# Forming w_out·phi with phi as the stationary operand in four column groups, and one more product that adds and transposes

## The chip, the cores and the metric

The kernel runs on one core of one Trainium2 chip. The metric is the device time of one execution in microseconds (us), lower is better. The matmul engine is called PE in the rows (PEld is its weight load), the vector engine DVE, the scalar engine ACT, GpSimd POOL, and the queue that issues DMAs SP.

## The reference

Three layers follow each other on 2304 tokens (4 sequences of 576) of 512 features. First comes an attention with 8 heads of 64, of which four see a local window of 32 positions and four every 32nd position; its output is `x`. Then a feed-forward layer and a soft mixture of experts:

```python
h = x @ w_in                                  # 2304x512 @ 512x2048
g = h * (1.0 / (1.0 + np.exp(-1.702 * h)))
x = g @ w_out                                 # 2048x512
logits = x @ phi                              # 512x32
d = softmax(logits, axis=0)                   # over the tokens
slot_input = d.T @ x                          # 32x512
# each of 8 experts: two products on its 4 rows of slot_input -> slot_out
c = softmax(logits, axis=1)                   # over the 32 slots
return c @ slot_out
```

The layer's output `x` (2304x512) is never needed by itself: `logits = g @ (w_out @ phi)`, and `slot_input = (d.T @ g) @ w_out`. The kernel therefore forms the small product `wp = w_out @ phi` (2048x32) once, and uses it as the weights of the logits.

## The kernel before, in words

The five chunks of tokens (`CHUNKS`, four of 512 and one of 256) go through a loop of 80 steps, `steps`, each step one chunk `c` and one of 16 slices `f` of 128 of the 2048 hidden features (`moe_step`, line 344). A step runs `gemm1` (line 304): twelve matmuls of 512 columns into `h` (line 311), then a tanh on ACT (line 314) and a product on DVE (line 315) that give `g`, kept in the slots of `gT`. Every fourth step `logits` (line 325) multiplies four slices of `g` by `wp` (line 330, four column groups of 32 side by side). `g_transpose` (line 333) turns `g` in DVE for the later product with the softmax weights.

While chunk 0 runs (steps 0 to 15), the weights are also prepared. `load_w(i + 2)` (line 251) reads the raw weights of a slice, which come as 64-bit numbers, and makes float32 of them: an ACT pass (line 259), a POOL pass (line 260) and three DVE passes (lines 261 to 263), for `w_in` (k = 0) and `w_out` (k = 1) each. `split(i + 1)` (line 266) cuts `w_in` into two parts, by an ACT cast (line 270) and a POOL subtraction (line 271), whose result `wi` the twelve matmuls of the step use. `wo_transpose(i + 1)` (line 273) transposes the slice of `w_out`, by four matmuls with the identity (line 278, the tile `wot`) and an ACT copy (line 280) to `woT`, four blocks of 128x128 with the 512 features on the partitions. `wo_phi(i)` (line 282) is what changes: it multiplies these four blocks, as the stationary operand, by `phs`, the four blocks of 128x32 of phi, as the moving one, and adds the four products in PSUM (line 286). An ACT instruction halves the 128x32 result into `wp[:, f]` (line 287).

The attention of the next sequence runs among these steps as well (`attention_steps`, resumed once a step through `side`): scores `s` (line 161, 64x64 operands), mask, maximum and exponential on DVE and ACT (lines 164 to 179), a POOL multiplication (line 182), transposes `ptp` (line 197) and products with the values `av` (line 216), whose results ACT and DVE move to `x` (lines 241 and 242).

The order of the work on each engine is not the order of the code: a scheduler lists the instructions by priority and readiness when the program is built. Each engine works through its list strictly in that order. The PSUM tiles `wp`, `wot`, `s`, `ptp` and `av` share one pool of five (`mtile`, line 65); `h` has two tiles of its own, and `lg` one. `sel` (line 85) is a constant 128x32 matrix whose row r has a one in column r mod 32.

Of the kernel before, what the change touches and what calls it, by code (L numbers as in the profile page):

```python
# [9 lines left out]
F32 = mybir.dt.float32  # L10
# [11 lines left out]
NS = NE * SPE  # L22
# [8 lines left out]
NF = FF // 128  # L31
# [10 lines left out]
def tile_kernel(ctx: ExitStack, tc: tile.TileContext, lqk, lv, sqk, sv, wraw, phi, wexp, cst, out):  # L42
    nc = tc.nc
    P = 128
# [16 lines left out]
    rawp = raw_es.enter_context(tc.tile_pool(name="rawp", bufs=3, side="right"))  # L61
# [3 lines left out]
    def mtile(name):  # L65
        return ps_m.tile([P, 512], F32, tag="m", name=name)
# [18 lines left out]
    sel = rep[:, :NS]  # L85
# [4 lines left out]
    phs = keep.tile([P, 4, NS], F32, name="phs")  # L90
    ca = keep.tile([P, NT // 128, NS], F32, name="ca")
    wp = keep.tile([P, NF, NS], F32, name="wp")
# [158 lines left out]
    def load_w(f):  # L251
        for k in range(2):
            if (f, k) not in raws:
                load_raw(f, k)
        for k in range(2):
            raw = raws.pop((f, k))
            t = rawp.tile([P, 512], F32, tag="wc", name=f"wc_{f}_{k}", bufs=4)
            u = t.bitcast(U32)
            nc.scalar.activation(t, raw[:, :, 1].bitcast(F32), AF.Abs)  # L259
            nc.gpsimd.tensor_scalar(t, t, F64_LARGE, F64_SMALL, op0=ALU.min, op1=ALU.max)  # L260
            nc.vector.tensor_scalar(u, u, 3, 0x3FFFFFF8, op0=ALU.logical_shift_left, op1=ALU.bitwise_and)  # L261
            nc.vector.scalar_tensor_tensor(u, raw[:, :, 1], 0xC0000000, u, op0=ALU.bitwise_and, op1=ALU.bitwise_or)  # L262
            nc.vector.scalar_tensor_tensor(u, raw[:, :, 0], 29, u, op0=ALU.logical_shift_right, op1=ALU.bitwise_or)  # L263
            conv[f, k] = t

    def split(f):
        if f % 2 == 0:
            wis[f // 2] = wip.tile([P, 2, 2, 512], F32R, tag="wi", name=f"wi_{f // 2}")
        w, t = wis[f // 2][:, f % 2], conv.pop((f, 0))
        nc.scalar.copy(w[:, 0], t)  # L270
        nc.gpsimd.tensor_tensor(w[:, 1], t, w[:, 0].bitcast(F32), op=ALU.subtract)  # L271

    def wo_transpose(f):
        t = conv.pop((f, 1))
        nc.sync.dma_start(wo_scr[f], t)
        tp = mtile(f"wot_{f}")
        for kt in range(4):
            nc.tensor.transpose(tp[:, 128 * kt:128 * kt + 128], t[:, 128 * kt:128 * kt + 128], ident)
        woT[f] = rawp.tile([P, 4, 128], F32, tag="woT", name=f"woT_{f}", bufs=1)
        nc.scalar.copy(woT[f].rearrange("p k f -> p (k f)"), tp)  # L280

    def wo_phi(f):
        t = woT.pop(f)
        pw = mtile(f"wp_{f}")[:, :NS]
        for kt in range(4):
            nc.tensor.matmul(pw, t[:, kt, :], phs[:, kt, :], start=kt == 0, stop=kt == 3)  # L286
        nc.scalar.mul(wp[:, f, :], pw, 0.5)

    steps = [(c, f) for c in range(len(CHUNKS)) for f in range(NF)]
    lgs, gs = {}, {}  # L290
# [13 lines left out]
    def gemm1(c, f):  # L304
        N = CHUNKS[c][1]
        x, w = xt[c], wis[f // 2][:, f % 2]
        h = ps_h.tile([P, 512], F32, tag="h", name=f"h_{c}_{f}")
        n = 0
        for kt in range(4):
            for we, xe in ((0, 0), (0, 1), (1, 0)):  # L310
                nc.tensor.matmul(h[:, :N], w[:, we, 128 * kt:128 * kt + 128], x[xe][:, kt, :N], start=n == 0, stop=n == 11)  # L311
                n += 1
        g = g_slot(c, f)
        nc.scalar.activation(g[:, :N], h[:, :N], AF.Tanh, scale=0.851)  # L314
        nc.vector.scalar_tensor_tensor(g[:, :N], g[:, :N], 1.0, h[:, :N], op0=ALU.add, op1=ALU.mult)  # L315
        gs[c, f] = g
# [8 lines left out]
    def logits(c, f0):  # L325
        N = CHUNKS[c][1]
        if f0 == 0:
            lgs[c] = ps_lg.tile([P, 512], F32, tag="lg", name=f"lg_{c}")
        for j in range(4):
            nc.tensor.matmul(lgs[c][32 * j:32 * j + 32, :N], wp[:, f0 + j, :], gs[c, f0 + j][:, :N], start=f0 == 0, stop=f0 == NF - 4)  # L330
            g_used(c, f0 + j)

    def g_transpose(c, f):
        N = CHUNKS[c][1]
        if c < 4:
            assert f not in taken
            taken.add(f)
        nc.vector.transpose(t_slots(c)[:, f, :N], gs[c, f][:, :N])  # L338
        g_used(c, f)
# [4 lines left out]
    def moe_step(i):  # L344
        c, f = steps[i]
        if i + 2 < NF:
            load_w(i + 2)
        if 0 < i < NF:
            wo_phi(i)
        for s in list(side):  # L350
            if next(s, True):
                side.remove(s)
        if i + 1 < NF:
            split(i + 1)
        if c == 0 or f >= TFROM:
            for _ in range(1 if c == 0 else 2):
                if todo and (c or todo[0][1] not in taken):
                    g_transpose(*todo.pop(0))
        while todo and todo[0][0] < c and todo[0][1] not in taken:
            g_transpose(*todo.pop(0))  # L360
        gemm1(c, f)
        if i + 1 < NF:
            wo_transpose(i + 1)
        if i and f % 4 == 0:
            pc, pf = steps[i - 4]
            logits(pc, pf)
            if f == 0:
                side.append(post(pc))
        todo.append((c, f))
# [147 lines left out]
    for n, _ in enumerate(attention_steps(0)):  # L517
        if n in (8, 12):
            load_w(n // 4 - 2)
        if n == 10:  # L520
            split(0)
    wo_transpose(0)
    wo_phi(0)
    busy_t[0] = cs.bitcast(BF16)[:, :512]
    early_es.close()
# [6 lines left out]
    for i, (c, f) in enumerate(steps):  # L532
        if f == 0 and c < 3:
            side.append(attention_steps(c + 1))
            next(side[-1])
        if (c, f) == (1, 0):
            raw_es.close()
            accp = acc_es.enter_context(tc.tile_pool(name="accp", bufs=1))
            sp_["p"] = accp
            acc = accp.tile([P, 4, 512], F32, name="acc")  # L540
            more = accp.tile([P, 3, 512], F32, name="more")
            slots.update({NF + 3 + k: more[:, k] for k in range(3)})
        if (c, f) == (3, 2):
            att_es.close()
            e1p = ctx.enter_context(tc.tile_pool(name="e1p", bufs=4, side="right"))
            for _ in range(4):
                load_ex(e1p, "e")
            for e in (1, 0, 1):
                load_ex(xp, f"x{e}")
        if (c, f) == (4, 1):  # L550
            for e in range(2):
                load_ex(xp, f"x{e}")
        moe_step(i)
        if (c, f) == (4, 4):
            for k in range(2):
                load_ex(None, gx_tile())
        if c == 4 and f % 2:
            load_ex(wip, "wi")
# [236 lines left out]
```

## Time and profile before

| | |
|---|---|
| median of 3 runs | 445.32 us (443.66 to 446.91) |
| the profiled execution, own time | 447.54 us |
| its span, first to last instruction | 445.7 us |
| mean granted TensorE clock in it | 0.973 |
| PE, DVE, ACT, POOL busy | 419.5, 263.4, 191.3, 77.4 us |

The rows further down are of that one execution; times in them are us from the start of its span, unless they are means of one instruction, which are ns. A row of PE gives records: one float32 matmul leaves two records (two passes). A record lasts from the start of an instruction to its end, and those of PE overlap, since the next one enters while the last one's results still drain.

### The profile page before, as it was taken

To read this page: it belongs to the slowest core of one execution; us is meant where nothing else is said; L and a number is where in the kernel's file an instruction comes from. 1 tells how busy PE (TensorE), PEld (TensorE's weight loads), DVE (VectorE), ACT (ScalarE), POOL (GpSimd) and SP (SyncE) were. 2 spreads that over 40 slices of the span, in tenths; PEclk is the share of its full clock that TensorE was granted. 3 is DMA by queue.
4 is the path that set the end of the run, shared out by engine and by line. 5 is a ranking of instruction groups with operands and counts; after the bars stand their busy time and mean duration, and the time that the engine had idled before them with its cause. 6 is when DMAs were issued, how large, how long until landed. Compare 5 with 4: busy or idle time off the path is not lost.

```text
span 445.7 us, 9998 instructions
## 1 busy us (share of the span) xinstructions
PE 419.5 (94%) x4056; PEld 294.1 (66%) x4056; DVE 263.4 (59%) x564; ACT 191.3 (43%) x623; POOL 77.4 (17%) x96
## 2 busy tenths in 40 slices
PE   8977999998879999999999999999999999899965
PEld 4546786766547776777775777776777796243655
DVE  2689899988975555555656556546544664431212
ACT  2785676756645553554552436331222222120312
POOL 0444445445451100010110001000000000010000
PEclk9999999999999999999999999999999999899985
DMA  8856667584762130212402101680002899879998
GB/s 244 352 162 221 217 194 275 175 287 159 248 219 65 57 95 4 92 36 79 166 25 73 37 2 37 225 341 1 1 0 89 304 368 329 338 290 427 421 351 249
DMA packets 25614, 80.90 MB, mean 181 GB/s; under 512 B 2144, under 2 KB 9440, under 8 KB 21472
## 3 DMA queue, kind: packets, MB, share of 16 engines
q1 hardware_dynamic: 25568, 80.26, 50.9%
q8 instruction: 32, 0.52, 0.5%
q14 instruction: 14, 0.11, 0.1%
HBM read 71.34 MB, written 8.91 MB: 180 GB/s over the span
## 4 chain that ended last, share of the span: by engine, by line
PE 73%; DVE 9%; DMA 6%; ACT 5%; POOL 4%; issue 2%; SPq 0%; ACTq 0%; POOLq 0%
PE h L311 41%; PE u L423 5%; PE s L161 4%; PE lg L330 4%; DMA out<-gT 4%; PE hp L627 3%; PE ptp L197 3%; DVE wc L262 3%; PE op L657 2%; PE wp L286 2%; PE av L216 2%; ACT ts L179 2%; DVE wc L263 2%; POOL wi L271 2%; DMA qk<-lqk 2%
## 5 line engine op out<-in xcount | busy, mean ns | idle before, releaser
L311 PE MATMUL h<-x,wi 128*128 128x512 f32 (+1 forms) x960 | 223.8, 380 | 5.9 <-POOL wi L271 3.5
L311 PEld LDWEIGHTS h<-x,wi 128*128 128x128 f32 x960 | 162.2, 189 | 53.4 <-issue 13.8
L315 DVE SCALAR_TENSOR_TENSOR gT<-gT,h 128x512 f32<-128x512 f32 (+1 forms) x64 | 40.5, 633 | 61.8 <-ACT gT L314 61.2
L314 ACT ACTIVATE gT<-h 128x512 f32<-128x512 f32 (+1 forms) x64 | 35.5, 555 | 69.7 <-PE h L311 69.4
L179 ACT ACTIVATE ts<-ts,nmx 128x64 f32<-128x64 f32 (+1 forms) x120 | 41.6, 349 | 29.1 <-DVE nmx L174 28.9
L182 POOL TENSOR_TENSOR ts<-ts,sm 128x384 f32<-128x384 f32 (+2 forms) x32 | 28.1, 880 | 138.7 <-DVE sm L181 63.7
L338 DVE STREAM_TRANSPOSE gT<-gT 128x512 f32<-128x512 f32 (+1 forms) x64 | 41.0, 649 | 0.8
L260 POOL TENSOR_SCALAR wc<-wc 128x512 f32<-128x512 f32 x32 | 24.1, 755 | 34.9 <-ACT wc L259 34.8
L262 DVE SCALAR_TENSOR_TENSOR wc<-raw,wc 128x512 uint32<-128x512 uint32 x32 | 28.0, 878 | 0.3
L263 DVE SCALAR_TENSOR_TENSOR wc<-raw,wc 128x512 uint32<-128x512 uint32 x32 | 26.6, 832 | 0.1
L161 PE MATMUL s<-qk 64*64 64x96 f32 (+1 forms) x552 | 26.0, 242 | 0.5 <-DMA qk<-lqk 0.5
L161 PEld LDWEIGHTS s<-qk 64*64 64x64 f32 x552 | 22.0, 138 | 6.6 <-issue 4.7
L330 PE MATMUL lg<-gT,wp 128*32 128x512 f32 (+1 forms) x128 | 26.4, 564 | 0.0
L271 POOL TENSOR_TENSOR wi<-wc,wi 128x512 fp32r<-128x512 f32 x16 | 22.5, 1407 | 14.7 <-ACT wi L270 14.3
L261 DVE TENSOR_SCALAR wc<-wc 128x512 uint32<-128x512 uint32 x32 | 17.2, 537 | 11.9 <-POOL wc L260 11.8
L201 ACT COPY pt<-ptp 96x384 f32<-96x384 f32 (+1 forms) x34 | 15.1, 483 | 20.3 <-PE ptp L197 20.1
L241 ACT CAST x<-av 128x320 fp32r<-128x320 f32 (+20 forms) x54 | 19.0, 398 | 10.5 <-DVE x L242 9.1
L180 DVE TENSOR_SCALAR sm<-sm 128x5 f32<-128x5 f32 (+2 forms) x32 | 7.1, 223 | 26.5 <-ACT ts L179 26.5
L423 PE MATMUL u<-gT,dT 32*32 32x512 f32 x576 | 21.1, 623 | 1.9 <-DVE z L398 1.9
L179 ACT ACTIVATION_READ_ACCUMULATOR ts<-ts,nmx 128x1 f32 x120 | 22.6, 188 | 0.0
L197 PE MATMUL ptp<-cs,ts 128*96 128x128 f32 (+1 forms) x120 | 18.1, 285 | 4.0 <-POOL ts L182 3.0
L259 ACT ACTIVATE wc<-raw 128x512 f32<-128x512 f32 x32 | 21.6, 678 | 0.7 <-DMA raw<-wraw 0.7
(120 smaller groups left out, 469.8 us busy)
## 6 DMA issues: line engine op xcount, KB each, us to landing
ex<-wexp SPq DMA_DIRECT2D x28, 1024.0 KB, 7.8
raw<-wraw SPq DMA_DIRECT2D x32, 512.0 KB, 3.7
qk<-lqk SPq DMA_DIRECT2D x8, 592.0 KB, 4.7
wo_scr<-wc SPq DMA_DIRECT2D x16, 256.0 KB, 2.4
ex<-wo_scr SPq DMA_DIRECT2D x4, 1024.0 KB, 9.5
gT<-wexp SPq DMA_DIRECT2D x4, 1024.0 KB, 5.9
qk<-sqk SPq DMA_DIRECT2D x6, 604.0 KB, 4.4
v<-lv SPq DMA_DIRECT2D x8, 432.0 KB, 4.4
```

Source lines behind the costliest of these rows:

```text
L161: nc.tensor.matmul(sp[hs, u], t[hs, qo:qo + 64], t[hs, ko + qo:ko + qo + nk], start=not early, stop=not early or u == nt - 1)
L179: nc.scalar.activation(ts[:, u], src[:, u], AF.Exp, scale=sc, bias=nmx[:, u:u + 1], accum_out=sm[:, u:u + 1])
L197: nc.tensor.transpose(ptp[:nk, u - a], src, ident)
L262: nc.vector.scalar_tensor_tensor(u, raw[:, :, 1], 0xC0000000, u, op0=ALU.bitwise_and, op1=ALU.bitwise_or)
L263: nc.vector.scalar_tensor_tensor(u, raw[:, :, 0], 29, u, op0=ALU.logical_shift_right, op1=ALU.bitwise_or)
L271: nc.gpsimd.tensor_tensor(w[:, 1], t, w[:, 0].bitcast(F32), op=ALU.subtract)
L311: nc.tensor.matmul(h[:, :N], w[:, we, 128 * kt:128 * kt + 128], x[xe][:, kt, :N], start=n == 0, stop=n == 11)
L314: nc.scalar.activation(g[:, :N], h[:, :N], AF.Tanh, scale=0.851)
L315: nc.vector.scalar_tensor_tensor(g[:, :N], g[:, :N], 1.0, h[:, :N], op0=ALU.add, op1=ALU.mult)
L330: nc.tensor.matmul(lgs[c][32 * j:32 * j + 32, :N], wp[:, f0 + j, :], gs[c, f0 + j][:, :N], start=f0 == 0, stop=f0 == NF - 4)
L338: nc.vector.transpose(t_slots(c)[:, f, :N], gs[c, f][:, :N])
L423: nc.tensor.matmul(us[a][32 * j:32 * j + 32, :].rearrange("p (t f) -> p t f", f=32), dT[q, 32 * b:32 * b + 32], gT[q, :, 32 * b:32 * b + 3 ...
```

## The change

`wo_phi` now loads a 128x32 block of phi as the stationary operand and streams the 128x128 block of `woT`. Each of the four blocks goes to a column group and to 32 PSUM partitions of its own, so the four products are not added: the result is 128x128, four transposed partial sums one below the other. ACT halves it into a new tile `wpT`. A new function `wo_phi_sum` then makes `wp[:, f]` by one product of `wpT` (stationary) with `sel`, which adds the four parts and transposes them, into a PSUM tile `wq` of the same pool, and by an ACT copy of 128x32. It is called one step later than the `wo_phi` of its slice, for the last slice in the first step of chunk 1.

```diff
+    wpT = {}
+
     def wo_phi(f):
         t = woT.pop(f)
-        pw = mtile(f"wp_{f}")[:, :NS]
+        pw = mtile(f"wp_{f}")[:, :P]
         for kt in range(4):
-            nc.tensor.matmul(pw, t[:, kt, :], phs[:, kt, :], start=kt == 0, stop=kt == 3)
-        nc.scalar.mul(wp[:, f, :], pw, 0.5)
+            nc.tensor.matmul(pw[32 * kt:32 * kt + 32], phs[:, kt, :], t[:, kt, :], start=True, stop=True)
+        wpT[f] = rawp.tile([P, P], F32, tag="wpT", name=f"wpT_{f}", bufs=2)
+        nc.scalar.mul(wpT[f], pw, 0.5)
+
+    def wo_phi_sum(f):
+        pw = mtile(f"wq_{f}")[:, :NS]
+        nc.tensor.matmul(pw, wpT.pop(f), sel, start=True, stop=True)
+        nc.scalar.copy(wp[:, f, :], pw)
...
         if 0 < i < NF:
             wo_phi(i)
+        if i <= NF and i:
+            wo_phi_sum(i - 1)
         for s in list(side):
```

The scheduler makes a new order from this. On PE, in the place of step 12 (`h_12`) of the kernel before, the product `wp` stands behind all of `h_12` and behind a logits matmul `lg`:

```order
L311 MATMUL h_12_1552<-x_0_302,wi_1477 128x512 x2
L278 MATMUL wot_1497<-cs,wc_1_1355 128x128 x4
L311 MATMUL h_12_1552<-x_0_303,wi_1477 128x512
L311 MATMUL h_12_1552<-x_0_302,wi_1477 128x512 x2
L311 MATMUL h_12_1552<-x_0_303,wi_1477 128x512
L311 MATMUL h_12_1552<-x_0_302,wi_1477 128x512
L330 MATMUL lg_983<-gT,wp 32x512
L286 MATMUL wp_1520<-phs,woT_1502 128x32 x4
L161 MATMUL s_3_1_1526<-qk_3_1367 64x64 x10
```

In the changed kernel the four `wp` matmuls (line 288) and the `wq` of the slice before (line 294) stand in the middle of `h_12`:

```order
L278 MATMUL wot_1542<-cs,wc_1_1392 128x128 x4
L319 MATMUL h_12_1601<-x_0_302,wi_1522 128x512 x2
L319 MATMUL h_12_1601<-x_0_303,wi_1522 128x512
L319 MATMUL h_12_1601<-x_0_302,wi_1522 128x512
L288 MATMUL wp_1565<-woT_1547,phs 32x128 x4
L294 MATMUL wq_1572<-cs,wpT_1485 128x32
L161 MATMUL s_3_1_1575<-qk_3_1408 64x64 x10
L319 MATMUL h_12_1601<-x_0_302,wi_1522 128x512
L319 MATMUL h_12_1601<-x_0_303,wi_1522 128x512
```

So `wp`, and the scores `s` behind it, have moved ahead of the rest of `h_12` and of `lg`. On ACT, in the same place, the kernel before has the tanh of `h_12` and the halving of `wp` ahead of the cast of `w_in` (line 270):

```order
L280 COPY woT_1502<-wot_1497 128x512
L314 ACTIVATE gT<-h_12_1552 128x512
L287 ACTIVATE wp<-wp_1520 128x32
L270 CAST wi_1477<-wc_0_1427 128x512
L259 ACTIVATE wc_0_1508<-raw_0_1504 128x512
```

In the changed kernel both new evictions stand ahead of that cast, and the tanh (line 322) behind it:

```order
L280 COPY woT_1547<-wot_1542 128x512
L259 ACTIVATE wc_1_1474<-raw_1_1466 128x512
L241 CAST x_2_897<-av_2_0_1490 128x18x4
L290 ACTIVATE wpT_1570<-wp_1565 128x128
L295 COPY wp<-wq_1572 128x32
L241 CAST x_2_897<-av_2_1_1491 128x14x4
L270 CAST wi_1522<-wc_0_1468 128x512
L322 ACTIVATE gT<-h_12_1601 128x512
L259 ACTIVATE wc_0_1553<-raw_0_1549 128x512
```

What ACT has to do before the cast is thus no longer the tanh of the whole step, but one eviction more.

## Rows read from the trace of the kernel before

**Rows 1.** The page: totals of engines, and busy tenths in 40 slices.

```profile
PE 419.5 (94%) x4056; PEld 294.1 (66%) x4056; DVE 263.4 (59%) x564; ACT 191.3 (43%) x623; POOL 77.4 (17%) x96
...
PE   8977999998879999999999999999999999899965
...
DVE  2689899988975555555656556546544664431212
```

**Rows 2.** Windows of 10 us, 40 to 150: busy time by engine, clock, DMA.

```profile
core 0: us, PE busy (x) PEld busy (x) DVE busy (x) ACT busy (x) POOL busy (x), PEclk, DMA share, GB/s
...
110.00:120.00 10.00, 8.82 (x84) 5.76 (x83) 10.00 (x19) 7.35 (x25) 5.94 (x6) 1.00 0.67 215
...
sum 110.00, PE 102.06 PEld 74.09 DVE 93.90 ACT 68.44 POOL 47.90; mean PE 9.28 PEld 6.74 DVE 8.54 ACT 6.22 POOL 4.35
```

**Rows 3.** The chain, pieces from 119 to 136: start, us, what.

```profile
120.92 1.02 PE wp L286 x8
...
122.75 1.29 POOL wi L271
...
128.09 1.02 PE wp L286 x8
```

**Rows 4.** The chain from 40 to 146, by line, share of it.

```profile
by line: PE h L311 22.5%; PE wp L286 9.5%; PE s L161 7.5%; POOL wi L271 7.2%; DVE wc L263 6.2%; DVE wc L262 6.1%; issue 5.2%; PE wot L278 5.1%; PE lg L330 4.6%; ACT ts L179 3.2%; PE ptp L197 3.1%; ACT wc L259 3.0%; POOL ts L182 2.4%; ACT pt
```

**Rows 5.** PE in order of time around two `wp` groups: start, us, records.

```profile
65.38 0.86 PE L311 MATMUL h<-x,wi 128*128 128x512 f32 x3
66.08 1.03 PE L286 MATMUL wp<-phs,woT 128*128 128x32 f32 x8
...
119.87 1.04 PE L330 MATMUL lg<-gT,wp 128*32 128x512 f32 x2
120.84 1.08 PE L286 MATMUL wp<-phs,woT 128*128 128x32 f32 x8
```

**Rows 6.** PE in order of time, single records at changes of tile shape.

```profile
93.73 0.39 PE L311 MATMUL h<-x,wi 128*128 128x512 f32 x1
94.05 0.62 PE L330 MATMUL lg<-gT,wp 128*32 128x512 f32 x1
...
94.50 0.59 PE L330 MATMUL lg<-gT,wp 128*32 128x512 f32 x1
95.03 0.50 PE L311 MATMUL h<-x,wi 128*128 128x512 f32 x1
...
426.30 0.43 PE L657 MATMUL op<-ex,hz 128*32 128x128 f32 x8
...
390.60 0.63 PE L586 MATMUL sip<-cs,acc_s 128*128 128x32 f32 x4
```

**Rows 7.** Groups of instructions by shape: busy us, mean ns of one.

```profile
L286 PE MATMUL wp<-phs,woT 128*128 128x32 f32 x128 | 16.8, 275 | 0.1
...
L657 PE MATMUL op<-ex,hz 128*32 128x128 f32 x256 | 8.6, 285 | 2.5 <-DMA ex<-wexp 2.5
```

**Rows 8.** ACT groups from 40 to 146 by shape: busy us, mean ns | idle before.

```profile
L287 ACT ACTIVATE wp<-wp 128x32 f32<-128x32 f32 x16 | 3.1, 196 | 9.6 <-PE wp L286 9.6
...
L241 ACT CAST x<-av 128x128 fp32r<-128x128 f32 x4 | 1.1, 265 | 0.0
```

**Rows 9.** Waits from 40 to 146 of PE, DVE and ACT: us, times, longest.

```profile
PE h L311 <- POOL wi L271: 3.5, 4, 1.2
PE h L311 <- ACT wi L270: 1.2, 2, 0.8
...
DVE wc L261 <- POOL wc L260: 8.9, 9, 2.3
...
ACT wp L287 <- PE wp L286: 9.6, 14, 1.4
```

**Rows 10.** A stretch at the lower clock, columns as in rows 2.

```profile
128.00:131.40 3.40, 1.83 (x11) 1.26 (x10) 3.20 (x8) 1.59 (x4) 1.48 (x1) 1.00 0.55 194
131.40:135.00 3.60, 3.31 (x10) 2.73 (x11) 1.81 (x3) 0.13 (x1) 1.50 (x3) 0.53 0.25 92
```

## The prediction

> **What bounds the kernel now.** I began with the page. Its first part shows PE busy for 94% of the span, and its slices show where PE is not full: at the start, at the end, and in slices 9 to 11, about 100 to 134 us, where DVE stands at eight or nine tenths [rows 1]. All sixteen `wp` groups lie between 41 and 143 us, so the second view is the windows of that stage. Of 110 us PE is busy 102.1, DVE 93.9 and ACT 68.4 [rows 2]: PE is nearly full, DVE has little room, ACT has some. Behind the stage PE is the bound almost to the end [rows 1], so what the stage gains or loses should arrive at the end nearly whole. Third, the chain of work in the stage: the `wp` products hold 9.5% of 106 us, 10.1 us [rows 4]; at 0.88 to 1.02 us a group that is 11 of the 16. The rest of the chain leaves PE and goes through the weight conversion: POOL's `wi` 7.2%, DVE's two `wc` passes 12.3%, ACT's casts [rows 4]. So PE's time counts in most of the stage, but not in all of it. Fourth, the waits: PE waits 3.5 us for POOL's `wi`, 1.2 for ACT's, and DVE waits 8.9 us for POOL's `wc` [rows 9].
>
> **PE, a step before.** An `h` group ends at 65.38 + 0.86 = 66.24, the eight `wp` records start at 66.08 and end at 67.11 [rows 5]. By ends, the block adds 0.87 us (the group row has 16.8 us for all sixteen, with the overlaps at both ends [rows 7]). Behind `lg` it adds more: `lg` ends at 120.91, `wp` at 121.92, 1.01 us [rows 5].
>
> **PE, a step after.** Two new shapes have near relatives in the trace. Eight records of 128x32 stationary and 128 moving columns, in four column groups, took 0.43 us from start to end when they followed another tile shape [rows 6]; in a long run of their own shape they cost 8.6 us / 256 = 34 ns each, 0.27 us for eight [rows 7]. The product with `sel` has the very form of `sip`: four records in 0.63 us [rows 6], 0.11 apart, so its two records last 0.41.
>
> A change of tile shape has a price that the trace shows. An `h` record ends at 94.12 and `lg` starts at 94.05; `lg` ends at 95.09 and `h` starts at 95.03 [rows 6]. So the next shape enters 0.07 before the end of the last record, where records of one shape enter 0.16 before it (66.24 and 66.08 [rows 5]): 0.09 us lost each way. Back in the full shape the first `h` record lasts 0.50 instead of 0.39 [rows 6], 0.11 for a weight load that nothing covers. The Trainium skill, in "TensorEngine Tiling (Array Packing)", section "Key Properties", says that changing the tiling mode drains the engine; the rows agree, with about 0.09 us a drain. The same page ("Performance Considerations") advises this very swap where the moving side has 32 columns or fewer, for up to 4x; by that alone the sixteen groups would give back three quarters of 14 us. The rows do not bear that out for a group this short, because of the drains and the second product.
>
> The sum by ends, behind `h`: the column groups add 0.43 - 0.07 = 0.36, and `wq`, which enters 0.06 before their end, adds 0.41 - 0.06 = 0.35. Together 0.71 against 0.87, so 0.16 saved. Behind `lg` no shape changes on the way in: 0.27 + 0.35 = 0.62 against 1.01, 0.39 saved. In the new order 12 of the 15 pairs `wp`, `wq` follow `h` and 3 follow `lg`: 12 x 0.16 + 3 x 0.39 = 3.1 us. The first `wp` has no `wq` behind it and saves 0.87 - 0.36 = 0.51; the last `wq` stands alone between two groups of scores and costs 0.35 and a further drain, 0.44. These cancel. From the first `wot` to the first `h` of chunk 1, the order has 66 changes of shape where there were 41, which is why so little of the 14 us is left as a gain. PE's work falls by 3.2 us.
>
> **Its bounds.** Without any price for changes of shape, a step would cost 0.27 + 0.22 against 0.89, and sixteen would give 6.4 us. If the column groups did not run side by side, eight records 0.11 apart would cost 0.88 by themselves and a step would lose about 0.4, 7 us in all. I take 3.2, since both halves of it were measured on records of the same shape.
>
> **ACT.** The halving grows from 128x32 (196 ns) to 128x128, for which the nearest PSUM read is 265 ns, and a copy of 196 ns is new [rows 8]: 0.27 us a step, 4.2 us in all, on an engine that is busy 62% of the stage [rows 2]. What hides it is that ACT stood idle 9.6 us for exactly this product, 14 of 16 times [rows 9]. While ACT waits, its path is PE's: before, 1.03 us of records and 0.20 of halving. After, 0.36 and 0.35 on PE from the same point, with the larger copy beside `wq`, then 0.20: some 0.2 us earlier. Where ACT does not wait, it is 0.27 later. With most steps in the first case I put ACT at nothing. Bounds: 16 x 0.2 = 3.2 us won, 4.2 lost.
>
> **Moves and waits.** `wq` waits for `wpT`, which was made a step earlier, so PE should not stop there; behind it stand `s`, `av`, `ptp` or `h`. The slices of `wp` are needed by `lg` later in the step and are one step later than before; the order has `lg` after them with `h` between. The fifth PSUM tile is now used where two `av` tiles, `wp`, `wq` and `s` live together; I cost a wait there at nothing to 0.3 us each at four places. SP moves one `qk` load of the next sequence behind one store and one raw load; its scores belong to chunk 1, and I put that at nothing. The order moves `wp` into the middle of `h_12` and `h_13`, ahead of `lg`; that is a term of its own, below.
>
> **Forecast.** Of PE's 3.2 us the part counts that lies on the chain, 11 of 16: 2.2 us. The profiled execution took 447.54 (span 445.7 and 1.8 around it); it stands 2.2 above the median of the runs. 445.3 - 2.2 gives **443.1 us** on the median's level. A measurement of this kernel can tell about 1%, 4.5 us, from no change, so this is a gain too small to be called one.
>
> **Rivals.**
>
> *The saving ends in another wait* (0.24). The stage is paced by the conversion: DVE is full from 110 to 120 [rows 2], and the chain spends a fifth of the stage in `wc` and `wi` [rows 4]. Then PE only arrives earlier at `wot`, which waits for DVE, or at `h`, which waits for POOL, and the 3.2 us turn up as idle time there. Against it: DVE has 16 idle us in the stage, 8.9 of them waiting for work that ACT starts. Time: 445.3, give or take 1.
>
> *The new order frees the conversion* (0.18). In two places the chain runs from `wp` behind `lg` to ACT, to its cast of `wi`, to POOL, and then PE stands [rows 3, 5]. In the new order `wp` precedes half of `h_12` and `lg`, and the cast no longer stands behind the tanh of that step. Half of the 4.7 us that PE waits for `wi` [rows 9] could go, and with it the stretch at the clock's lower level, 131.4 to 135 us (granted 0.53, with PE busy 1.83 of 3.4 us just before it), in which 3.3 us of work would have taken 1.7 at the upper level [rows 10]. 443.1 - 2.4 - 1.6 = 439.1. Against it: DVE works nearly without a pause there (3.2 of 3.4 us [rows 10]), and its conversions end no earlier because PE is ready for them.
>
> *ACT becomes the one that is late* (0.14), the slower side. The place is ACT's list, where both evictions stand ahead of the cast of `wi`, and where the raw weights' first pass waits too. Each step then hands the conversion on 0.27 later, 16 x 0.27 = 4.2, and PE's saving does not count as the chain is not on PE: 445.3 + 4.2 = 449.5; with one more stretch at the lower clock 451. It decides from the point at which ACT no longer waits for `wp` (the 9.6 us fall under some 4). The Trainium skill, same page, "PSUM Bottleneck", warns of this: tiling speeds up the matmuls but not the reading of PSUM. The trace has room on ACT, but not everywhere (7.35 of 10 us at 110 to 120 [rows 2]).
>
> *The groups do not run side by side* (0.02): 445.3 + 7 = 452. Eight such records in 0.43 us speak against it.
>
> **The numbers.** The forecast has 0.42, its own spread 440.5 to 445.5. Faster by over 1% (under 440.9) takes most of the freed conversion, 0.16, and the edge of the forecast, 0.06: 0.22. Slower by over 1% (over 449.8) takes half of the ACT case, the last rival and some of a worse order: 0.12. Within 1%: 0.66. The range that leaves out two in ten is 438.8 to 449.
>
> **What would show it.** Right: the `wp` records at line 288 about 0.43 us a group with the four groups starting together, `wq` 0.4, both together busy under 13 us against 16.8 [rows 7]; the first `h` of chunk 1 two to three us earlier; ACT's waiting for PE at lines 290 and 295 together no more than 9.6 us; PE idle in the stage no more than 1 us above before. Wrong: PE's waits for `wi` or for DVE's `wc` growing by 3 us (the first rival) or falling by 2 (the second); ACT busier with no waits at line 290 and `wi` later (the third); a wait of PE at `wq`.

## The result, and the profile after

The changed kernel takes **442.43 us** (median of 13 runs, 440.57 to 443.76), the kernel before 446.38 in the same comparison (13 runs, 443.66 to 450.61). The ratio is 0.9909, 95% interval 0.9889 to 0.9929: 4 us faster, 0.9%. The profiled execution took 442.75 us, its span is 441.0.

The page after, totals and the same two slices as [rows 1], and then the sum over the windows from 40 to 150 us [rows 2].

```profile
PE 410.5 (93%) x4082; PEld 282.8 (64%) x4088; DVE 264.9 (60%) x564; ACT 195.3 (44%) x639; POOL 78.5 (18%) x96
...
PE   8877898998989999999999999999999998999965
...
DVE  2689999998987454565466535546454654431212
```

```profile
sum 110.00, PE 99.17 PEld 67.27 DVE 96.69 ACT 75.78 POOL 50.54; mean PE 9.02 PEld 6.12 DVE 8.79 ACT 6.89 POOL 4.59
```

PE is busy 2.9 us less in these 110 us, DVE 2.8 and ACT 7.3 more. Part of that is only that chunk 1 begins earlier in this window. So the next view cuts out the same work in each kernel: from the first `h` of step 1 to the first `h` of chunk 1. Chunk 1 begins at 145.65 us before and at 140.44 after. The two windows, columns as in [rows 2], of before and then of after:

```profile
46.30:145.65 99.35, 92.53 (x735) 66.62 (x733) 85.27 (x155) 62.90 (x187) 45.50 (x48) 0.98 0.61 202
```

```profile
44.46:140.44 95.98, 86.28 (x767) 58.22 (x766) 87.72 (x159) 66.96 (x203) 46.46 (x49) 1.00 0.64 214
```

The stage is 3.4 us shorter, and PE works 6.2 us less in it. The other 2.9 us are PE's idle time, which grew from 6.8 to 9.7. About half of the 6.2 is the smaller product; of the rest, some is the stretch at the lower clock, 131.4 to 135 us before [rows 10], which this execution does not have (1.00 in the clock column).

The new product, single records after (the places of [rows 5, 6]) and then the groups from 40 to 146 us (of [rows 7, 8]):

```profile
121.25 1.17 PE L319 MATMUL h<-x,wi 128*128 128x512 f32 x4
122.35 0.43 PE L288 MATMUL wp<-woT,phs 128*32 128x128 f32 x8
122.71 0.41 PE L294 MATMUL wq<-cs,wpT 128*128 128x32 f32 x2
122.95 1.17 PE L319 MATMUL h<-x,wi 128*128 128x512 f32 x4
...
128.03 0.87 PE L197 MATMUL ptp<-cs,ts 128*128 128x128 f32 x6 [1.64 <-POOL ts L182]
```

```profile
L288 PE MATMUL wp<-woT,phs 128*32 128x128 f32 x128 | 7.3, 284 | 1.7 <-ACT woT L280 1.5
L294 PE MATMUL wq<-cs,wpT 128*128 128x32 f32 x32 | 6.5, 287 | 0.0
L290 ACT ACTIVATE wpT<-wp 128x128 f32<-128x128 f32 x16 | 4.4, 274 | 1.8 <-PE wp L288 1.5
L295 ACT COPY wp<-wq 128x32 f32<-128x32 f32 x16 | 2.9, 180 | 1.0 <-PE wq L294 0.7
```

Eight records last 0.43 us, `wq` 0.41: the four column groups run side by side. The waits after, for comparison with [rows 9]:

```profile
PE ptp L197 <- POOL ts L182: 5.0, 5, 1.6
...
DVE wc L261 <- POOL wc L260: 4.2, 8, 1.1
...
ACT wpT L290 <- PE wp L288: 1.5, 4, 0.7
...
PE lg L338 <- ACT wp L295: 0.6, 1, 0.6
```

PE's 4.7 us of waiting for `wi` are gone from PE's rows altogether. In their place PE waits 5.0 us for `ts`, the attention's multiplication on POOL; one of these waits is at 128.03 above. DVE's waiting for POOL's `wc` fell from 8.9 to 4.2. The chain from 40 to 146, the view of [rows 4]:

```profile
by line: DVE wc L262 11.3%; PE h L319 10.2%; DVE wc L263 10.1%; issue 8.8%; DVE wc L261 7.0%; POOL wc L260 5.1%; ACT ts L179 4.6%; POOL ts L182 3.9%; ACT wc L259 3.5%; PE s L161 3.1%; DVE gT L323 3.0%; DVE ts L164 2.9%; DVE nmx L174 2.5%; D
```

Before, `h` held 22.5% and `wp` 9.5%, and DVE's passes stood behind them. After, the three DVE passes of the weight conversion hold 28.4%, `h` 10.2%, and `wp` is not among the lines listed, which end at 2.5%. The path that was second is now the first.

### The profile page after: what moved, and what is told of

Its sections match the earlier page's. It is cut to its first block, busy times and chain, and to the rows that moved or that the text cites. A ratio compares the mean times of both kernels' runs of the same rounds, so it can differ in the third digit from the quotient of the medians.

```text
span 441.0 us, 10075 instructions
## 1 busy us (share of the span) xinstructions
PE 410.5 (93%) x4082; PEld 282.8 (64%) x4088; DVE 264.9 (60%) x564; ACT 195.3 (44%) x639; POOL 78.5 (18%) x96
## 4 chain that ended last, share of the span: by engine, by line
PE 67%; DVE 15%; ACT 6%; DMA 4%; POOL 4%; issue 3%; ACTq 0%; POOLq 0%
PE h L319 37%; PE u L433 5%; DMA out<-gT 4%; DVE wc L262 4%; PE lg L338 4%; PE s L161 3%; PE hp L637 3%; ACT ts L179 3%; DVE wc L263 3%; PE op L667 2%; PE ptp L197 2%; DVE wc L261 2%; PE av L216 2%; POOL wc L260 2%; PE busy L78 2%
## 5 line engine op out<-in xcount | busy, mean ns | idle before, releaser
L319 PEld LDWEIGHTS h<-x,wi 128*128 128x128 f32 x960 | 161.8, 189 | 47.1 <-issue 13.8
L262 DVE SCALAR_TENSOR_TENSOR wc<-raw,wc 128x512 uint32<-128x512 uint32 x32 | 26.8, 839 | 0.3
L263 DVE SCALAR_TENSOR_TENSOR wc<-raw,wc 128x512 uint32<-128x512 uint32 x32 | 26.7, 835 | 0.2
L161 PE MATMUL s<-qk 64*64 64x96 f32 (+1 forms) x552 | 25.0, 236 | 0.2 <-DMA qk<-lqk 0.2
L161 PEld LDWEIGHTS s<-qk 64*64 64x64 f32 x552 | 20.9, 134 | 6.4 <-issue 4.9
L180 DVE TENSOR_SCALAR sm<-sm 128x5 f32<-128x5 f32 (+2 forms) x32 | 8.6, 268 | 26.7 <-ACT ts L179 26.7
L197 PEld LDWEIGHTS ptp<-cs,ts 128*96 128x96 f32 (+1 forms) x120 | 12.8, 132 | 16.8 <-POOL ts L182 13.6
L261 DVE TENSOR_SCALAR wc<-wc 128x512 uint32<-128x512 uint32 x32 | 18.6, 584 | 7.2 <-POOL wc L260 7.1
L179 ACT ACTIVATION_READ_ACCUMULATOR ts<-ts,nmx 128x1 f32 x120 | 22.5, 187 | 0.0
```

The source lines that it names most:

```text
L161: nc.tensor.matmul(sp[hs, u], t[hs, qo:qo + 64], t[hs, ko + qo:ko + qo + nk], start=not early, stop=not early or u == nt - 1)
L179: nc.scalar.activation(ts[:, u], src[:, u], AF.Exp, scale=sc, bias=nmx[:, u:u + 1], accum_out=sm[:, u:u + 1])
L197: nc.tensor.transpose(ptp[:nk, u - a], src, ident)
```

## The experiments

Three theories stood against each other. **The product**: PE's saved time lies on the path at eleven sixteenths, and is the gain. **The other wait**: the stage is paced by the weight conversion, and PE's saving becomes idle time. **The order**: the gain comes from where the scheduler now puts the instructions, above all ACT's cast of `wi`.

To separate product and order, most of these kernels have their issue order written down: a list of instructions for each engine, and a helper that chains neighbours without any semaphore or wait.

```diff
+def hold_order(tc):
...
+        for a, b in zip(names, names[1:]):
+            tc.add_manual_dep(by[b], a, first, reason="order")
```

### The helper itself, and product and order apart

`before_again` is the kernel before with its own order written down.

> The kernel before, with every engine's issue order written down and held to what it already was: the same program once more. Both theories: ratio 1.000 within 0.003, about 446.4 us. Its trace answers whether the two stretches at the lower clock (42.9 and 131.6 us) belong to the program. If they do, both come again and the mean clock is 0.973 again. If they hang on where an execution happens to fall, at least one is missing or elsewhere and the clock is 0.977 or more.

Measured: 446.39 us, ratio 0.9991 (0.9966 to 1.0015). Holding an order costs nothing that can be told, so the next two can be read against before. Of the two stretches at the lower clock, the one at 42.9 us is missing in its trace, and the other stands at 130.9 us. Its profiled execution took 444.33 us, 2.1 less than the median of its runs.

`old_product_new_order` has the old product (line 286) in the place of the new one, and on every engine the changed kernel's order for all else.

> The product of the kernel before (four accumulating matmuls, one eviction of 128x32), every other instruction on each engine in the order of the changed kernel, the old group and its eviction in the places of the new ones. If the order brought the gain (wp ahead of half of h_12 and h_13, the cast of wi ahead of the tanh): about 443, ratio 0.993 or below, PE's waits for wi in steps 12 to 15 gone. If the cheaper product brought it: 446, ratio 1.000, or above that if the new order suits only the short product. If each brought half: 444.5, ratio 0.9955.

Measured: 442.99 us, ratio 0.9916 (0.9891 to 0.994). That is 3.7 us of the 4.0, with not one matmul saved, and PE's waits for `wi` are gone from its rows. In this order the product adds only 0.3 us, with an interval of some 1.4 us each side. The stage as profiled is 1.3 us shorter than that of `before_again` (98.97, below), and still 1.7 longer than after:

```profile
45.40:143.03 97.63, 91.69 (x735) 66.82 (x734) 86.07 (x157) 62.82 (x187) 44.94 (x48) 0.98 0.63 210
```

This execution has a stretch at a granted clock of 0.50 (1.2 GHz) from 116.4 to 119.8 us, and that of after has none in the stage. So single executions do not settle the shares, and the medians of the runs are the better guide.

`new_product_old_order` has the new product and its sum, and for all else the order of before; `wq` and its copy come in at the next place where they fit.

> The new product (column groups, wq, two evictions), every other instruction in the order of the kernel before; wq of the slice before and its copy stand directly ahead of the new group and its halving, or ahead of the logits that need them. If the order brought the gain: 445.5 to 446.5, ratio 0.998 to 1.000, with PE's idle time in the stage larger by what its work fell (3 us) and PE still waiting 3 to 5 us for wi. If the product brought it: 442.5 to 443.5, ratio 0.992. If half each: 444.5.

Measured: 444.64 us, ratio 0.9961 (0.994 to 0.9982). This is the time that was expected if each brought half: the product without the new order gives 1.7 us (0.8 to 2.7). So the two gains do not simply add. The product is worth 1.7 us in the old order and 0.3 in the new one; the order is worth 3.7 us without the product and 2.3 with it (from 0.9961 to 0.9909). The order has the larger part both ways, though 1.7 against 2.3 us lies within the noise. The stage, in `before_again` and then in this kernel, cut as above:

```profile
44.85:143.82 98.97, 92.33 (x736) 66.88 (x734) 86.37 (x157) 62.85 (x187) 45.63 (x48) 0.98 0.61 207
```

```profile
44.59:143.56 98.97, 87.55 (x767) 59.81 (x765) 86.57 (x159) 65.58 (x203) 45.19 (x49) 1.00 0.61 207
```

PE is busy 4.8 us less and the stage has the same length to the hundredth: in these two executions the difference became idle time. Not all of the 4.8 is the product. `before_again` has a stretch at 0.50 from 130.9 to 134.3 us in which PE is busy throughout, and this execution has none; an estimate from that, half of those 3.4 us, is 1.7 us. The waits say where PE stands:

```profile
PE lg L338 <- ACT wp L295: 3.5, 5, 1.2
PE h L319 <- POOL wi L271: 3.3, 5, 0.8
PE wot L278 <- DVE wc L263: 2.2, 3, 1.1
```

The stage speaks for the other wait, with a reservation: in this order `wq` stands just ahead of `lg` in some steps, and the 3.5 us at `lg` are a cost of that place, not of the product. So the run may understate what the product is worth alone. The 1.75 us by which its median is below that of `before_again` don't come from the stage as profiled. Its runs had a higher mean clock (0.983 in the median, against 0.980 for `before_again` and 0.977 for before), which may be the source; no run shows it. The same holds for the order: `old_product_new_order` has 0.9815 against that 0.977. As an estimate, 0.004 of 445 us is 1.8 us, so a good part of each gain can be clock, and these runs do not separate it from the waits.

### Fewer products

`pairs` forms `wp` for two slices at once: 64 partitions hold one half of the sum over the features for both slices, so that half as many 128x128 results, sums and evictions are left. `sel2` adds two parts instead of four, and `woT` has two buffers. The scheduler orders it as it likes.

```diff
-        for kt in range(4):
-            nc.tensor.matmul(pw[32 * kt:32 * kt + 32], phs[:, kt, :], t[:, kt, :], start=True, stop=True)
+        for k in range(2):
+            for h in range(2):
+                for j in range(2):
+                    o = 64 * h + 32 * j
+                    nc.tensor.matmul(pw[o:o + 32], phs[:, 2 * h + k, :], ts[j][:, 2 * h + k, :], start=k == 0, stop=k == 1)
...
+        nc.tensor.matmul(pw, wpT.pop(f0), sel2, start=True, stop=True)
```

> Two slices at a time: the four column groups hold two slices times two halves of the 512 features, each group adds two blocks in PSUM, one product with a 128x64 selection gives both slices, one copy of 128x64 follows. Half the changes of shape, half the evictions (16 instead of 32), the same streaming. If PE's work or ACT's evictions pace the stage: PE about 1.5 us less than in the changed kernel, ACT about 3 us less, 440.5 to 442. If the conversion on DVE and POOL paces it: 442.4, the same as the changed kernel, or up to 2 us either way by the new order.

Measured: 445.89 us, ratio 0.9987 (0.9963 to 1.0012), a miss: it lies outside both expectations. It has less work on PE and ACT than the changed kernel (753 PE records in the stage against 767, ACT busy 64.2 us against 67.0), and none of the gain. PE waits 3.6 us for POOL's `wi` and 1.3 for ACT's in it, as before the change. That fits the order, and does not fit the product; but its order is one more new one, so the run alone proves neither.

### Which part of the order

`late_new_order` and `early_new_order` have the old product. On each engine the first has the order of before up to the end of `h_11` on PE and the new order from there; the second has it the other way round.

> Product of the kernel before; every engine in the old order up to the end of step 11 on PE (and the matching places on the other engines), in the new order from there. If the gain of the new order lies in steps 12 to 15 (wp ahead of half of h_12 and h_13, the cast of wi earlier): 443 to 443.6, ratio 0.992 to 0.9935, the wait of PE for wi there under 0.5 us. If it lies in the steps before, or is spread evenly: 445 or more, ratio 0.997 to 1.000.

Measured: 444.19 us, ratio 0.9955 (0.9929 to 0.9981), between the two expectations.

> The counterpart: new order up to step 11, old order from there, old product. If the gain lies in the late steps: 446 to 446.5, ratio 0.999 to 1.001, with the waits for wi and the stretch at the lower clock near 131 us back. If it lies in the early steps: 443 to 444.

Measured: 447.10 us, ratio 1.0021 (0.9994 to 1.0047), with PE's waits for `wi` (2.5 and 0.8 us) and a stretch at the lower clock at 131.3 us back. The new order of steps 12 to 15, less than a third of the stage (115.03 to 145.65 us before), gives some 2 us by itself; that of the first twelve steps gives nothing by itself. Both together give 3.7, so the two are not simply added; that is left open.

### One cast, moved twice

Steps 12 and 13 are where the chain of before left PE [rows 3]. In the kernel before, ACT and the conversion there (ACT in order of time, then DVE's third pass, whose result the cast reads):

```profile
119.98 0.60 ACT L314 ACTIVATE gT<-h 128x512 f32<-128x512 f32 x1 [0.52 <-PE h L311]
121.96 0.20 ACT L287 ACTIVATE wp<-wp 128x32 f32<-128x32 f32 x1 [1.39 <-PE wp L286]
122.06 0.61 ACT L270 CAST wi<-wc 128x512 fp32r<-128x512 f32 x1
...
129.13 0.20 ACT L287 ACTIVATE wp<-wp 128x32 f32<-128x32 f32 x1 [0.82 <-PE wp L286]
129.23 0.61 ACT L270 CAST wi<-wc 128x512 fp32r<-128x512 f32 x1
```

```profile
119.29 0.93 DVE L263 SCALAR_TENSOR_TENSOR wc<-raw,wc 128x512 uint32<-128x512 uint32 x1
...
127.95 0.68 DVE L263 SCALAR_TENSOR_TENSOR wc<-raw,wc 128x512 uint32<-128x512 uint32 x1
```

The weights were ready at 120.22 and 128.63, the casts began at 122.06 and 129.23: 1.84 and 0.60 us late, behind a halving for which ACT stood waiting for PE. `cast_ahead` is the kernel before, its order written down, with these two casts ahead of the tanh and the halving, and nothing else moved:

```diff
+L270 CAST wi
 L314 ACTIVATE gT<-h
 L287 ACTIVATE wp<-wp
-L270 CAST wi
```

> The kernel before in its own order, but for two moves on ACT: in steps 12 and 13 the cast of w_in (line 270) stands ahead of the tanh of the step and of the halving of wp, not behind them. If ACT's list is what holds the conversion back there: PE's wait for wi at 122 us goes and the one at 128 to 130 shrinks by half, the stretch at the lower clock near 131 mostly goes, 444 to 445, ratio 0.994 to 0.997. If the place of wp on PE matters by itself, or DVE is late anyway: 446 to 446.5, ratio 0.999 or more.

Measured: 443.63 us, ratio 0.9937 (0.9913 to 0.9962). Two moves on ACT, no engine's work changed, 2.8 us by the ratio (1.7 to 3.9). ACT, and then PE, in that kernel:

```profile
120.91 0.62 ACT L270 CAST wi<-wc 128x512 fp32r<-128x512 f32 x1 [0.81 <-DVE wc L263]
121.43 0.59 ACT L314 ACTIVATE gT<-h 128x512 f32<-128x512 f32 x1
```

```profile
123.22 2.11 PE L311 MATMUL h<-x,wi 128*128 128x512 f32 x8
...
129.19 0.73 PE L311 MATMUL h<-x,wi 128*128 128x512 f32 x2 [0.39 <-ACT wi L270]
130.54 1.40 PE L311 MATMUL h<-x,wi 128*128 128x512 f32 x5 [0.63 <-POOL wi L271]
```

The cast now waits for DVE, not for PE. The same places on PE in the kernel before:

```profile
122.72 0.73 PE L311 MATMUL h<-x,wi 128*128 128x512 f32 x2
124.08 1.66 PE L311 MATMUL h<-x,wi 128*128 128x512 f32 x6 [0.63 <-POOL wi L271]
...
129.89 0.73 PE L311 MATMUL h<-x,wi 128*128 128x512 f32 x2 [0.79 <-ACT wi L270]
131.69 0.80 PE L311 MATMUL h<-x,wi 128*128 128x512 f32 x1 [1.07 <-POOL wi L271]
```

All eight records of `h` from 123.22 run through, where PE stopped for `wi` between the second and the third; the two waits near 130 us shrank from 0.79 and 1.07 to 0.39 and 0.63. The stretch from 131.4 to 135 us, half at the lower clock before [rows 10], has the full clock:

```profile
131.40:135.00 3.60, 3.48 (x22) 2.50 (x21) 2.19 (x5) 2.50 (x6) 1.95 (x3) 1.00 0.27 106
```

What the moves give shows in steps 12 to 15, counted by the twelve matmuls of `h` in each. `before_again` and then `cast_ahead`:

```profile
113.60:143.82 30.22, 26.04 (x209) 19.05 (x207) 22.67 (x42) 15.51 (x41) 11.94 (x12) 0.94 0.50 168
115.68:143.41 27.73, 24.59 (x209) 17.55 (x207) 22.93 (x42) 15.68 (x41) 11.93 (x12) 1.00 0.56 183
```

They are 2.5 us shorter, as much as in the changed kernel (27.86 us). PE idles 1.0 us less, and the same work keeps it busy 1.5 us less, at the higher clock. But the trace of `cast_ahead` has a stretch at the lower clock elsewhere, in steps whose order was not touched:

```profile
103.00:106.40 3.40, 3.40 (x14) 3.11 (x13) 2.05 (x4) 2.11 (x4) 0.32 (x2) 0.50 0.57 209
```

The same waits of PE (0.44, 0.63 and 0.49 us) stand ahead of it there and in `before_again`, whose clock stayed at 1.00 at that place. So as profiled the whole stage is only 0.7 us shorter (98.29 against 98.97). That the waits shrink is shown; how often the stretch falls away with them is not. The mean clock of the runs speaks for it (0.984 in the median, against 0.980 for before).

`casts_ahead_all` does the same in all seven steps in which a tanh or a halving stood directly ahead of the cast.

> The old product in the old order, but on ACT the cast of wi (line 270) moved ahead of the tanh and of the halving of wp in all seven steps in which one of them stood directly ahead of it (the run cast_ahead moved two of these). If the cast behind ACT's list is what the late stage waits for, the other five give something more: 442.5 to 443.5 us. If the two steps with the waits for wi were all, the same as cast_ahead, 443.6. If the moved casts stop ACT, because DVE has not finished the weights they read, and hold up the halving behind them, 445 to 447.

Measured: 445.57 us, ratio 0.9969 (0.9945 to 0.9993). The other five moves add nothing, and perhaps cost something (the intervals overlap). In steps 12 and 13 ACT stands still for DVE in it, as it does in `cast_ahead` (0.81 and 0.85 us):

```profile
121.72 0.62 ACT L270 CAST wi<-wc 128x512 fp32r<-128x512 f32 x1 [1.00 <-DVE wc L263]
...
129.35 0.62 ACT L270 CAST wi<-wc 128x512 fp32r<-128x512 f32 x1 [0.87 <-DVE wc L263]
```

A cast ahead of its weights helps nothing: behind ACT's list the next limit is DVE. In its profiled execution the stretch at the lower clock near 132 us is there again (granted 0.50 from 132 to 134 us), and its runs have a mean clock of 0.979 in the median, against 0.984 for `cast_ahead`. What the five moves cost and what the clock did is not separated.

### The waits that came instead

`turn_later` is the changed kernel with its own order, but the transposes `ptp` of steps 6, 10 and 14, where PE waited most for `ts`, stand behind four more matmuls of `h`.

> The changed kernel in its own order, but on PE in steps 6, 10 and 14 the transposes ptp stand behind four more matmuls of h. Its trace has PE wait for POOL's ts at these places for 1.18, 1.16 and 1.64 us with those matmuls ready behind it. If PE's idle time in this stage counts: 2 to 3.5 us less, 439 to 440.5, ratio to the kernel before 0.984 to 0.987. If DVE's conversions set the pace by now: the idle time moves to wot or wi, and it is 441.5 to 442.5, ratio 0.989 to 0.991.

Measured: 442.78 us, ratio 0.9923 (0.9895 to 0.9951), no better than the changed kernel. PE's waits in it:

```profile
PE wp L288 <- ACT woT L280: 3.7, 5, 1.0
PE wot L278 <- DVE wc L263: 1.6, 2, 0.9
...
PE ptp L197 <- POOL ts L182: 1.1, 2, 0.8
```

The wait for `ts` fell from 5.0 to 1.1 us and turned up at `woT` (1.5 us after) and `wc` (0.8 after). It was not a cause, only where PE's spare time is seen.

`after_casts_ahead` moves the cast ahead of both evictions and the tanh in six steps of the changed kernel.

> The changed kernel's own order, but on ACT the cast of wi moved ahead of both evictions (lines 290, 295) and of the tanh in the six steps in which they stood directly ahead of it. If the cast is still late in some steps, 440.5 to 441.8 us. If the changed kernel's waits for wi are already gone, as its trace shows (none of 0.6 us or more), the same as the changed kernel within 0.8 us, 441.6 to 443.2. If the cast now keeps wp from logits, up to 444.

Measured: 443.14 us, ratio 0.991 (0.9886 to 0.9933): the same as the changed kernel. In the changed kernel the two casts for `h_13` and `h_14` are no longer late: they begin 0.03 and 0.04 us behind the DVE pass that they read.

### What PE's time is worth

`wq_thrice` prices PE's time in the changed kernel's order, with each `wq` done three times, into the same tile:

```diff
-        nc.tensor.matmul(pw, wpT.pop(f), sel, start=True, stop=True)
+        t = wpT.pop(f)
+        for k in range(3):
+            nc.tensor.matmul(pw, t, sel, start=True, stop=True)
```

> The changed kernel with its issue order written down, and each product wq (the selection product) done three times into the same tile, so that PE has 4 more records in each of 16 steps and nothing else changes on any engine. Two wq records last 0.41 us and enter 0.11 apart, so PE's work in the stage grows by 16 x 4 x 0.11 = 7 us. If eleven sixteenths of PE's time in the stage lie on the path, as the prediction had it, the kernel takes 442.4 + 4.8 = 447.2 us. If all of it lies there, 449.5. If the stage is paced by the weight conversion and PE has slack in it, most of the 7 us goes into PE's idle time (about 7 us between the first h and the first h of chunk 1) and the time is 442.4 to 444.5.

Measured: 445.71 us, ratio 0.9978 (0.9961 to 0.9995), between the two. Its group and its stage:

```profile
L296 PE MATMUL wq<-cs,wpT 128*128 128x32 f32 x96 | 13.7, 280 | 0.0
```

```profile
45.16:142.82 97.66, 92.47 (x831) 65.27 (x828) 86.55 (x159) 66.65 (x203) 44.96 (x49) 1.00 0.64 210
```

The group grew by 7.2 us, from 6.5. In the stage PE works 6.2 us more than after, its idle time falls by 4.5 (from 9.7 to 5.2), and the stage is 1.7 longer: 27% arrives. By the ratios, 0.9978 against 0.9909, 3.1 us of the 7.2 arrive, 43%, with an interval of some 1.2 us each side. Eleven sixteenths would be 5.0 us.

### A version in plain source

`cast_first_after` writes no order down: the changed kernel with `split` called ahead of `wo_phi`.

```diff
+        if i + 1 < NF:
+            split(i + 1)
         if 0 < i < NF:
             wo_phi(i)
         if i <= NF and i:
             wo_phi_sum(i - 1)
...
-        if i + 1 < NF:
-            split(i + 1)
```

> The changed kernel with two lines of the source in another order, no order written down: split(i+1), which issues the cast and the subtraction of wi, is called ahead of wo_phi and wo_phi_sum instead of behind them, and the scheduler makes its own order from that. If the cast's priority is what the order's gain comes from, it keeps the gain, 441 to 443.5 us. If the new order of the rest (scores, transposes, evictions) matters more, it can fall anywhere between the changed kernel and the one before, 443.5 to 446.5.

Measured: 442.24 us, ratio 0.9906 (0.9886 to 0.9926). It keeps the gain and adds nothing that can be told from it. The order that the scheduler made is nearly that of the changed kernel: on ACT the casts keep their places, and only one `wp` copy and one tanh stand elsewhere in the stage. So the run is close to a repeat, and does not test the cast's priority. No run here was better than the changed kernel by more than its interval.

## Why the prediction was right or wrong

The time, 443.1 against 442.4, and the case (within 1%) came out. The way to it did not, and that the time is so near is in part luck. The forecast started from 445.3, the median of three runs, where before has 446.4 in the comparison: the gain forecast was 2.2 us, the gain measured 4.0.

**The step that failed** is "Of PE's 3.2 us the part counts that lies on the chain, 11 of 16: 2.2 us", as the whole of the sum, with nothing for the new order beside it. In the order that the changed kernel has, the product gives 0.3 us by the ratios (`old_product_new_order` 0.9916, the changed kernel 0.9909), with an interval of some 1.4 us each side, so 2.2 lies outside. `wq_thrice` shows that 27 to 43% of PE's added time arrives there; as an estimate, that makes 0.9 to 1.4 us of 3.2. In the old order the product gave 1.7 us (0.8 to 2.7), which does not speak against 2.2. And the order, which the sum had at nothing, gave 2.3 to 3.7 us. A share of the chain says what lay on it, not what is gained by shortening it: a second path, DVE's conversion, ran beside it, and the chain after the change runs through it (28.4%). The prediction had noted that the chain left PE for a fifth of the stage, and then used only the part that it held.

**What gave the time instead** is the rival *the new order frees the conversion*, to which it had given 0.18. The order without the product gives 3.7 us, and two moved casts give 2.8. The rival named the place (the two steps), the way (ACT's cast no longer behind the tanh, with the wait for PE ahead of it) and the two parts (the waits for `wi`, the stretch at the lower clock). The first part is shown; the second is open, since the trace of `cast_ahead` has such a stretch at another place. The prediction's own sign for this rival came: PE's waits for `wi` fell by more than 2 us, from 4.7 to none listed. Its size was off: it put 4.0 us on top of the 2.2. Counted by the twelve matmuls of `h` in each, the steps 12 to 15 are shorter by 2.4 us (from 143.82 - 113.60 in `before_again` to 140.44 - 112.58), and the steps 1 to 11 by 0.6. Its counter-argument, that DVE works nearly without a pause there, was half right: DVE is the next limit, but it lay 1.84 and 0.60 us behind the point where ACT began.

**The rival *the saving ends in another wait*** holds for the product in part: PE's idle time in the stage grew from 6.8 to 9.7 us, where the prediction allowed 1, and in the old order the stage got no shorter as profiled. By the runs the product still gave 0.3 to 1.7 us. The rival failed as a forecast of the time because the order came on top.

**PE's sizes.** One reading was off: in slice 11 DVE stands at seven tenths, not eight or nine [rows 1]. `wp` 0.43 and `wq` 0.41 us were as estimated from [rows 6]. The two groups together are busy 13.8 us, not under 13; the prediction's own lengths already make 16 x (0.43 + 0.41) = 13.4. The fall of PE's work, 3.2 us forecast, shows as 2.9 in the 40 to 150 us window, which is not quite the same work. In the rows above `wp` enters 0.07 us before the end of `h`, and `wq` 0.07 before the end of `wp`, where the shape changes; `h` enters 0.17 before the end of `wq`, where it does not. By ends the pair adds 0.70 us, as forecast (0.71). The Trainium skill, "TensorEngine Tiling (Array Packing)", section "Performance Considerations", gives 4x column tiling for a stationary side of 32 columns. The trace does not bear that out: eight records went from 1.03 [rows 5] to 0.43 us, and with the second product the pair adds 0.70 where 0.87 stood.

**ACT at nothing.** Right in the sum. In the stage ACT is busy 4.1 us more (62.90 to 66.96), as the 4.2 bound had it, and its waiting for the two products is 2.2 us against 9.6 before. That is below the 4 us from which the rival *ACT becomes late* was to decide, and it did not come: the evictions now wait little for PE, and the larger ones fit into the time in which ACT had stood.

**The moves.** `wq` never stopped PE. The fifth PSUM tile and the moved `qk` load show no wait of their own. A new wait of `lg` for `wp`, 0.6 us once, was not foreseen. The four groups ran side by side, as expected.

**What it should have done.** The two terms had been put as alternatives, a forecast and a rival, though nothing made them exclude each other. The runs show that they do not simply add either (the product 1.7 us in the old order, 0.3 in the new one). With the product at a third (1.1) and the freed conversion at the rival's 4.0 the sum would have been a gain of 5.1 us, where 4.0 was measured and 2.2 forecast.

## What to carry to other kernels

A share of the chain says what lies on it, not what a shorter step gives: look at what runs beside it before the share is taken, here an engine that was full in the same windows. When a change makes a scheduler order anew, hold the old order with the new work and the new order with the old work; two runs then say what each moves alone, and whether the two add. And in an engine's list look for an instruction whose input is long ready but which stands behind one that waits for another engine: moving two such casts was worth 2.8 us here, and the rewritten product 0.3 to 1.7.

## What the runs showed of the hardware

**One program, with and without a stretch at the lower clock.** The first `h` of step 1 starts at 46.30 us in the profiled execution of before and at 44.85 in that of `before_again`, which is the same program in the same order. From 40 to 46 us, before and then `before_again`:

```profile
40.00:46.00 6.00, 4.88 (x49) 4.47 (x49) 5.44 (x12) 2.67 (x7) 2.02 (x2) 0.74 0.48 160
```

```profile
40.00:46.00 6.00, 4.87 (x57) 4.10 (x56) 6.00 (x13) 3.50 (x9) 1.99 (x2) 1.00 0.45 159
```

PE is busy for equally long, the granted clock is 0.74 in the mean of the one (part of it at 1.2 GHz) and 1.00 (2.4 GHz) in the other, and eight records fewer get done. So of the 4.7 us between the spans of the two profiled executions, before and after, 1.5 are not the change's. The changed kernel has a stretch near 375 us (0.66 from 374 to 379 us). The profiled execution of before has one at nearly the same place of its work, 6 us later, and that of `before_again` has none there:

```profile
380.80:384.20 3.40, 3.40 (x56) 0.81 (x40) 1.29 (x2) 1.07 (x2) 0.00 (x0) 0.50 0.63 236
```

Over all profiled executions there is a pattern that nothing here explains. The seven with the old product each have at least one stretch at 0.50 between 40 and 150 us, in whatever order. The six with the new product, `pairs` left aside, have none there, the one in the old order included; four of them have one near 375 us. So it cannot be put down to the order alone that the stretch at 131.4 us is gone after the change.

**DVE's passes get longer when POOL runs.** The three DVE passes of the conversion, in the kernel before (minimum, median, maximum ns):

```profile
L261 DVE TENSOR_SCALAR wc<-wc x32: 382/427/1403, 19.4 to 137.1; 128x512 uint32<-128x512 uint32 x32
L262 DVE SCALAR_TENSOR_TENSOR wc<-raw,wc x32: 643/692/1704, 19.8 to 137.6; 128x512 uint32<-128x512 uint32 x32
L263 DVE SCALAR_TENSOR_TENSOR wc<-raw,wc x32: 643/684/1761, 22.8 to 139.8; 128x512 uint32<-128x512 uint32 x32
```

The same operation on the same shape takes 2.5 to 3.3 times its median at most. Set beside POOL's instructions, the 48 passes that overlap none of them are at most 10 ns over their median; the 48 that overlap one are together 14.6 us over it (after, 52 passes: 15.1, of which 11.4 in the stage). One is the pass from 123.11 to 124.58 us, 1.47, with POOL's `wi` at 122.75 for 1.29 [rows 3] beside it. The Trainium skill, "SBUF — State Buffer", section "SBUF: two separate sides", says that the vector engine, in operations with two inputs or in a two-port mode, and GpSimd share a pair of ports that one of them locks for a whole instruction; the trace agrees, with those 14.6 us. This is on the engine that paces the stage, and the 11.4 us are more than PE's idle time there (9.7 us after). No kernel here took POOL's work away from it, so what it is worth in time is open.
